# Gate weights loaded ahead of the second half of chunk 1's decay factors, and the steps of the first third in a new order

## The chip, the core and the metric

The kernel runs on one NeuronCore of a Trainium2 chip. That core has five engines, each with its own in-order instruction queue: TensorE (PE, matrix products), VectorE (DVE), ScalarE (ACT), GpSimd (POOL) and SyncE (SP, which here only issues DMAs). POOL both computes and issues DMAs. The metric is the device time of one execution in microseconds; the number of a kernel is the median of its runs.

## The reference

Two stages follow each other. The first is a gated linear recurrence over 768 positions, for 4 sequences with 8 heads of width 48; the second is a bilinear feed-forward layer over the 3072 tokens that come out of it.

```python
for t in range(S):                                     # S = 768
    state = alpha[:, :, t, :, None] * state + einsum('bhd,bhe->bhde', k[:, :, t], v[:, :, t])
    y[:, :, t] = einsum('bhd,bhde->bhe', q[:, :, t], state)
x = y.transpose(0, 2, 1, 3).reshape(B * S, H * D)      # 3072 x 384
a = x @ w_a                                            # 384 x 1536
b = x @ w_b                                            # 384 x 1536
out = (a * b) @ w_out                                  # 1536 x 384
```

## The kernel before

**Tiling.** The work is cut into six chunks, 0 to 5. A chunk is two of the four sequences (called u = 0 and u = 1) times 256 positions, 128 rows with a pair of positions in each. Chunks 0 and 1 are the first 256 positions of all sequences, 2 and 3 the next, 4 and 5 the last. Within a chunk the recurrence is computed in two halves g = 0 and 1 of 64 rows: logarithms of alpha are summed by a triangular matrix product, exponentials of the sums scale q and k, scores are formed, masked and multiplied with v, and the state carried from before is added. After that the chunk's 512 tokens go through the feed-forward layer, in 12 slices f of 128 columns of each of w_a and w_b.

**What sets the order.** No scheduler does. One string, `PROGRAM` (line 17), lists every step by hand in the form `chunk: step; step; ...`, and each engine gets its own steps in that order. A step waits for the data that it reads, and for the buffers and PSUM banks that it writes to be free; whatever stands behind it on its engine waits too. The last letter of many steps names the engine (V DVE, S ACT, P POOL, Y SP). A number at the end of a PE step is its PSUM bank (0 to 7); some steps take that bank and the next one.

The steps that matter here:

- `ld x u E`: DMA of chunk's a (alpha), q, k or v for u (`*` both, 0a/0b half the heads) from engine E's queue. `W a lo hi`, `W b lo hi`, `Wo lo hi`: DMA of columns of w_a, w_b, slices of w_out, all on POOL's queue.
- `ln u` (ACT, L554): logarithm of alpha. `l2 u P` (L562): sum of the two logarithms of a pair. `H`, `L` (DVE, L599, L605) and `R` (L621): splits of it into parts for PE. `B u` (PE, L589 and L590, two banks), `A2` (L636), `AQ` (L631, two banks): the running sums. `E u i`, `E u b` (ACT, L665): exponentials. `ra` (ACT, L643), `lv` (L650): scalings with single decay factors.
- `mk`, `mq` (DVE, L676): scaled k and q. `C u h` (PE, L736): their transposes; `Ce` (L960 on DVE, L958 on ACT): out of PSUM. `D u h` (PE, L837, two banks): scores; `M` (DVE, L846), or `Mc` (ACT, L850) and `Mm` (DVE, L854): scores masked.
- `dk` (PE, L698) and `de` (ACT, L719): decay over half a chunk. `K u g`, `K2` (PE, L792, L805): contribution of k and v to the state. `k u g V` (DVE, L819; L822 and L823 for g = 1): the new state.
- `v`, `vs` (L769 or L771; L958 or L960): v cast and its rows swapped. `SB`, `Y`, `SA` (PE, L866): the chunk's output, in two banks; `X` (L902 on ACT, L904 on DVE) takes it out as the input of the feed-forward layer.
- `a f u`, `b f u` (PE, L921): a slice of x @ w_a or x @ w_b for the tokens of u, three products over 256 columns, or of both (`*`), three over 512. `as` (ACT, L927) copies the a slice out of PSUM, into one of three buffers; `pr` (DVE, L935) multiplies it with the b slice. `o m half` (PE, L943): half of the product with w_out for 128 tokens; `ot` (L958) and `st`: out.
- `cz`, `cs`, `c2`, `c3`, `cm`, `ci`, `cu`: constants and zeros, mostly on POOL.

Chunks overlap: while chunk 0 is in its feed-forward layer, chunk 1's alphas, keys and queries go through ACT, DVE and POOL, and chunk 2's inputs are loaded. Around the change the DMA order on POOL's queue was: chunk 0's v, a, k, q for u = 1, then `W b 0 256`, `ld v 1`, `W a 256 768`, `W a 0 256`, `W b 256 512`, `W b 512 768`, chunk 1's `ld a 0` and `ld a 1`, `W a 768 1536`, `W b 768 1536`, chunk 1's `ld q 0`, `ld k 0`, `ld v 0`, `l2 0 P` (a computation), `ld q 1`, `Wo 0 6`, `l2 1 P`, `lv 0 q P`, `ld k 1`, `Wo 6 12`, then chunk 2's `ld a *` and so on.

Of the kernel before, what the change touches and what calls it, by code (L numbers as in the profile page):

```python
# [55 lines left out]
0: a 8 * 6; pr 5 1; pr 10 *
1: E 0 b
0: a 7 * 0; b 7 * 2
1: mq 0 V
0: b 11 * 4  # L60
2: ld k * P
1: lv 0 k V; E 0 i; mk 0 V
0: as 11 *; pr 11 *; a 6 * 3; as 7 *
1: A2 1 0
3: ld v * P
1: E 1 b
0: cz 1 v P; c3 P; pr 7 *
1: E 1 i
0: as 6 *; pr 6 *
1: dk * 7; de *  # L70
0: a 9 * 5; as 9 *; b 8 * 0
1: C 0 1 7; mq 1 V; Ce 0 1 V; C 0 0 2
0: b 9 * 1; pr 9 *; o 2 0 3; as 8 *; pr 8 *
1: Ce 0 0 S; D 0 0 4; Mc 0 0; K2 0 0 2 6
0: o 0 0 7; o 3 0 0
1: k 0 0 V; k 0 1 V; SB 0 4
3: ld a * P
1: mk 1 V; D 0 1 1; M 0 1
0: o 3 1 -; ot 3 V; st 3 Y
1: v 0 S; vs 0 0 S; vs 0 1 S; Mm 0 0 V; C 1 1 6; Ce 1 1 V  # L80
2: ln *
0: o 0 1 -; ot 0 S
1: C 1 0 2; Ce 1 0 S; v 1 V; vs 1 0 S
0: o 1 0 0; o 1 1 -; ot 1 S
# [12 lines left out]
2: R 0
1: D 1 0 6; as 4 0; k 1 0 V
2: ra 0
1: SB 1 2  # L100
2: R 1
1: k 1 1 V
2: AQ 0; E 1 i; ld v * P; E 1 b
1: pr 2 0; a 10 0 4; as 10 0; a 7 0 5; M 1 0; a 1 0 6; Mm 1 1 V; b 4 0 7; pr 4 0; b 1 0 1; a 5 0 4; as 1 0
1: pr 1 0
2: lv 0 q P; E 0 b; dr
1: b 10 0 6; pr 10 0; a 6 0 7; as 7 0; b 7 0 1; pr 7 0; b 5 0 5; as 5 0
# [5 lines left out]
1: b 6 0 1
2: mk 1 V; E 0 i
1: as 6 0; a 0 0 0; b 0 0 7; pr 6 0; a 11 0 4; X 1 S; a 2 1 5; b 3 0 2; as 0 0; pr 0 0; as 11 0; a 3 0 3
1: as 3 0; a 8 0 4; b 9 0 0; b 2 1 1; a 6 1 3; pr 11 0; as 2 1; a 9 0 5; as 9 0; pr 3 0; o 2 0 2
3: ln *; l2s 0 P; l2 0 P
0: st 0 Y
1: a 5 1 5; pr 2 1
2: lv 0 k V  # L120
1: as 8 0; a 8 1 1; as 8 1; b 8 0 6; a 3 1 7; pr 9 0; a 10 1 0
2: mk 0 V
1: pr 8 0
2: T 1
1: b 8 1 4; pr 8 1; b 5 1 1
2: dl
1: as 5 1; pr 5 1
3: l2s 1 P
1: as 6 1; b 6 1 6; pr 6 1; as 3 1; b 3 1 3; pr 3 1
# [1048 lines left out]
```

## Time and profile before

| what | value |
|---|---|
| median of 3 runs | 188.94 us (188.89 to 191.47) |
| the profiled execution: its own time | 190.44 us |
| the profiled execution: span from first to last instruction | 188.7 us |
| mean granted clock of TensorE | 0.991 |
| DVE busy | 152.6 us (81% of the span) |
| ACT busy | 120.1 us (64%) |
| POOL busy | 53.6 us (28%) |
| DMA moved | 29.43 MB |

Times in the profile count from the first instruction of the execution. "Busy" of PE includes the time a product spends in the pipeline, so a busy PE need not be at its full rate; the distance between the starts of neighbouring products shows the rate. A line of the timeline gives the start, the duration, the engine, the code line and operation, the output and input tiles and the number of merged instructions; a bracket at its end gives the idle time of the engine before it and who ended that.

### The profile page before, as it was taken

What the parts mean: (1) busy time and instruction counts of PE and PEld (TensorE: products, weight loads), DVE (VectorE), ACT (ScalarE), POOL (GpSimd) and SP (SyncE); (2) the same over time, 40 slices, a digit from 0 to 9 for tenths busy, and PEclk for the clock granted to TensorE, in tenths of its full rate; (3) what the DMA queues carried; (4) which work ended last, traced back from release to release, by engine and by line L of the source; (5) the groups of instructions that cost most, each with busy time, mean ns of one, the idle gap of its engine ahead of it and who ended that gap; (6) DMA issues with size and microseconds to landing.
All of it is one profiled execution on the core that took longest, in us unless ns stands there. A gap on an engine that the chain in (4) does not pass through costs nothing.

```text
span 188.7 us, 6347 instructions
## 1 busy us (share of the span) xinstructions
PE 181.9 (96%) x2693; PEld 122.3 (65%) x2709; DVE 152.6 (81%) x271; ACT 120.1 (64%) x228; POOL 53.6 (28%) x74
## 2 busy tenths in 40 slices
PE   7979999999999999999999999999999999999993
PEld 3969886566778886754445644555457477565992
DVE  2484889788979799998889899999999945696862
ACT  4364865579995797797697949965980451526230
POOL 8999654998062240003500003300000000000000
PEclk9987999999999999999999999999999999999999
DMA  5999999999999899989999699939500102110053
GB/s 125 263 225 195 261 235 254 230 231 257 247 214 129 129 215 276 275 237 182 198 173 271 144 116 167 112 107 165 89 0 9 43 0 83 44 43 0 0 170 127
DMA packets 66285, 29.43 MB, mean 156 GB/s; under 512 B 55776, under 2 KB 64624, under 8 KB 66256
## 3 DMA queue, kind: packets, MB, share of 16 engines
q1 hardware_dynamic: 47488, 16.34, 41.2%
q0 software_dynamic: 18624, 12.58, 39.3%
q8 instruction: 21, 0.34, 0.7%
q10 hardware_dynamic: 144, 0.10, 0.2%
q14 instruction: 8, 0.07, 0.1%
HBM read 25.98 MB, written 4.74 MB: 163 GB/s over the span
## 4 chain that ended last, share of the span: by engine, by line
PE 90%; ACT 6%; issue 2%; DVE 1%
PE psum L921 47%; PE psum L943 12%; PE psum L1032 11%; PE psum L866 5%; PE psum L837 3%; PE psum L589 2%; PE psum L590 2%; PE psum L736 2%; PE psum L572 2%; ACT vx L958 2%; PE psum L631 1%; ACT la L554 1%; PE psum L792 1%; PE psum L805 1%; PE psum L698 1%
## 5 line engine op out<-in xcount | busy, mean ns | idle before, releaser
L921 PE MATMUL psum<-xT,wb_t 128*128 128x512 bf16 (+1 forms) x263 | 55.8, 336 | 0.5 <-issue 0.2
L921 PE MATMUL psum<-xT,wa_t 128*128 128x512 bf16 (+1 forms) x262 | 55.2, 335 | 0.5 <-issue 0.2
L921 PEld LDWEIGHTS <-wa_t 128*128 128x128 bf16 x270 | 25.7, 98 | 19.2 <-issue 0.5
L921 PEld LDWEIGHTS <-wb_t 128*128 128x128 bf16 x270 | 25.5, 98 | 18.4 <-issue 0.5
L943 PE MATMUL psum<-wo_t,prod 128*128 128x384 bf16 x144 | 26.1, 327 | 0.0
L958 ACT ACTIVATE ot<-psum 128x384 f32<-128x384 f32 (+1 forms) x23 | 11.2, 487 | 17.7 <-PE psum L1032 15.4
L650 POOL TENSOR_TENSOR q_t<-q_t,ra 128x384 f32<-128x384 f32 x6 | 6.4, 1072 | 53.6 <-ACT ra L643 31.1
L943 PEld LDWEIGHTS <-prod 128*128 128x128 bf16 x144 | 13.3, 98 | 8.3
L958 ACT ACTIVATE vx<-v_t 32x384 bf16<-32x384 bf16 x26 | 13.5, 521 | 1.5 <-DVE vx L771 1.1
L1032 PEld LDWEIGHTS <-prod 128*128 128x128 bf16 x144 | 12.0, 98 | 1.2
L850 ACT ACTIVATE m<-psum 128x768 bf16<-128x768 f32 x14 | 11.0, 810 | 2.3 <-PE psum L837 2.3
L676 DVE TENSOR_TENSOR QKp<-q_t,beta 128x768 bf16<-128x768 f32 x10 | 9.4, 952 | 1.9 <-ACT beta L665 1.6
L554 ACT ACTIVATE la<-a_t 128x1536 f32<-128x1536 f32 (+2 forms) x9 | 9.5, 1054 | 1.7 <-DMA a_t<-in_alpha_dram 1.5
L676 DVE TENSOR_TENSOR QKp<-k_t,invb 128x768 bf16<-128x768 f32 x10 | 10.1, 1013 | 0.3
L846 DVE TENSOR_TENSOR m<-psum,mask 128x768 bf16<-128x768 f32 x10 | 9.5, 949 | 0.6 <-PE psum L837 0.6
L1044 DVE TENSOR_TENSOR ot<-psum,ot 128x384 f32<-128x384 f32 x9 | 5.0, 555 | 5.9 <-issue 3.2
L866 PE MATMUL psum<-m,vx 64*64 64x128 bf16 (+1 forms) x576 | 8.7, 205 | 0.0
L547 POOL DMA_DIRECT2D v_t<-in_v_dram x8 | 8.5, 1064 | 0.0
L866 PE MATMUL psum<-kqT,Sm 64*64 64x128 bf16 x144 | 7.5, 220 | 0.4 <-DVE Sm L819 0.4
L866 PEld LDWEIGHTS <-vx 64*64 64x64 bf16 x576 | 7.6, 108 | 0.1
L854 DVE TENSOR_TENSOR m<-m,mask 128x768 bf16<-128x768 bf16 x14 | 7.4, 550 | 0.0
L665 ACT ACTIVATE prod<-psum 128x384 f32<-128x384 f32 x8 | 3.5, 488 | 6.0 <-PE psum L590 6.0
(292 smaller groups left out, 361.5 us busy)
## 6 DMA issues: line engine op xcount, KB each, us to landing
out_dram<-ot SPq DMA_DIRECT2D x23, 192.0 KB, 2.7
q_t<-in_q_dram SPq DMA_DIRECT2D x3, 768.0 KB
k_t<-in_k_dram SPq DMA_DIRECT2D x3, 768.0 KB
a_t<-in_alpha_dram POOLq DMA_DIRECT2D x2, 768.0 KB, 11.7
v_t<-in_v_dram POOLq DMA_DIRECT2D x4, 384.0 KB, 7.6
a_t<-in_alpha_dram SPq DMA_DIRECT2D x2, 768.0 KB
a_t<-in_alpha_dram POOLq DMA_DIRECT2D x3, 384.0 KB, 7.5
k_t<-in_k_dram POOLq DMA_DIRECT2D x3, 384.0 KB, 7.3
```

The lines of the kernel that those rows point to most:

```text
L547: eng.dma_start(out=t[:, us, hs].rearrange("p b h r d -> p (b h) (r d)"), in_=src[ch.b0 + us.start:ch.b0 + us.stop, hs, ch.s * 2 * C:(ch.s ...
L554: nc.scalar.activation(out=ch.la[:, us, hs].rearrange("p b h r d -> p (b h r d)"), in_=ch.a[:, us, hs].rearrange("p b h r d -> p (b h r d) ...
L650: eng.tensor_mul(x, x, by)
L676: eng.tensor_mul(QKp[ch.c % 2][:, u, j, :, hs, :D], src[:, u, hs].rearrange("p h r d -> p r h d"), f)
L846: nc.vector.tensor_mul(m, x, maskn())
L850: nc.scalar.activation(out=m, in_=x, func=AF.Copy)
L854: eng.tensor_mul(m, m, maskn())
L866: nc.tensor.matmul(o, lhsT=lhsT, rhs=rhs, start=(g, c) not in begun, stop=False, skip_group_check=True)
L921: nc.tensor.matmul(p, lhsT=(wa_t, wb_t)[w][:, kk, f * 128:(f + 1) * 128], rhs=ch.xT[:, kk, us, :], start=(kk == 0), stop=(kk == KT - 1))
L943: nc.tensor.matmul(op, lhsT=ch.prod[:, f, at:at + C], rhs=wo_t[:, f, :], start=(f == 0), stop=(f == NFF - 1))
L958: nc.scalar.activation(out=o_, in_=i_, func=AF.Copy)
L1032: nc.tensor.matmul(o[:, g], lhsT=A[:, f, g * C:(g + 1) * C], rhs=W[:, f], start=(not more and (apart or g == 0) and f == 0), stop=(f == LH ...
```

## The change

The set of 893 steps is the same in both programs. `PROGRAM` is new between its third line and the step `o 2 0 2` of chunk 1's feed-forward layer: order and PSUM banks of the steps, on PE, ACT and DVE. From there to the end the program is unchanged but for some banks. On POOL's queue two things move: `W a 0 256` goes ahead of `W a 256 768`, and chunk 1's `ld a 1` goes behind `W a 768 1536`, `c2 P` and `W b 768 1536`. SP's queue keeps its order. In chunk 0, `K 0 1` and `dk 1` go ahead of chunk 0's running sums for u = 1 (`B 1a`, `B 1b`), and `ln 1` goes ahead of `vs 0 0 S`; in chunk 1, u = 0 goes ahead of u = 1 in more steps than before.

```diff
-0: E 0b i; mk 0b V; ld k 1 P; ld q 1 P; cm 1; W b 0 256; cz 0 v P; E 0b b; mq 0b V; ld v 1 P; W a 256 768; dk 0 2
-0: C 0 1 3; E 0a i; mk 0a V; cz 1 q P; E 0a b; mq 0a V; v 0 S; Ce 0 1 V; fill 2 0; W a 0 256; de 0; W b 256 512
-0: C 0 0 1; Ce 0 0 V; D 0 1 2; K 0 0 0; vs 0 0 S; W b 512 768; cs 1 m P
+0: E 0b i; mk 0b V; ld k 1 P; ld q 1 P; cm 1; W b 0 256; cz 0 v P; E 0b b; mq 0b V; ld v 1 P; W a 0 256; dk 0 2
+0: C 0 1 3; E 0a i; mk 0a V; cz 1 q P; E 0a b; mq 0a V; v 0 S; Ce 0 1 V; fill 2 0; C 0 0 4; Ce 0 0 V; D 0 1 0
+0: M 0 1; de 0; W a 256 768; K 0 0 3; D 0 0 5; k 0 0 V; K 0 1 2; ln 1; dk 1 4; de 1; vs 0 0 S; SB 0 0
+0: B 1a 3; E 1a i; k 0 1 V; M 0 0; vs 0 1 V; E 1a b; B 1b 5; W b 256 512; E 1b i; mk 1a V; mq 1a V; C 1 0 7
+0: Y 0; SA 0; mk 1b V; E 1b b; K 1 0 2; W b 512 768; mq 1b V; cs 1 m P
 1: ld a 0 P
-0: D 0 0 4; k 0 0 V; SB 0 0; M 0 0; ln 1; B 1a 6
-1: ld a 1 P
-0: W a 768 1536; c2 P; W b 768 1536; E 1a i; E 1a b; B 1b 4
-1: ld q 0 P
-0: dk 1 6
-1: ld k 0 P
-0: vs 0 1 V; E 1b i; M 0 1; Y 0; mk 1a V; mq 1a V; mk 1b V; SA 0; E 1b b; mq 1b V; C 1 0 7; Ce 1 0 V
-0: K 1 0 2; C 1 1 3; de 1; k 1 0 V; Ce 1 1 V
...
+0: C 1 1 3; Ce 1 0 V; v 1 S; vs 1 1 V; vs 1 0 V; D 1 0 4; X 0 S; b 1 0 7; Mc 1 0; a 1 0 6; as 1 0; b 0 0 0
+0: a 3 0 1; a 2 0 4; Ce 1 1 V; D 1 1 5; as 3 0; k 1 0 V; SB 1 1; K 1 1 3; as 2 0; a 0 0 4; pr 1 0; a 5 0 7
+0: Mm 1 0 V; k 1 1 V; Mc 1 1; Mm 1 1 V; a 4 0 3; b 3 0 5; W a 768 1536; pr 3 0; SA 1; as 5 0; Y 1; b 5 0 5
+0: b 4 0 6; b 2 0 7; X 1 V; as 0 0; pr 5 0; a 2 1 4; pr 2 0; c2 P; a 3 1 1
+1: ln 0
+0: W b 768 1536; pr 0 0; as 2 1; a 4 1 2; as 4 1; b 4 1 7; b 2 1 0; pr 2 1; b 3 1 4; b 0 1 2; as 3 1; pr 3 1
+0: a 0 1 1; b 1 1 0; b 5 1 4; as 4 0; pr 4 0; a 1 1 3
+1: ra 0
+0: pr 4 1; as 0 1; pr 0 1; a 7 * 5; a 5 1 1; as 5 1; a 11 * 6; b 7 * 7; b 10 * 1
+1: ld a 1 P; ld q 0 P; ld k 0 P
+0: as 1 1; b 11 * 2; as 11 *
+1: ld v 0 P; l2 0 P
+0: a 10 * 3; pr 5 1; a 9 * 4; as 7 *
+1: H 0 V; L 0 V; ld q 1 P; A2 0 5
...
+1: ln 1
+0: as 10 *; pr 7 *; pr 10 *
+1: E 0 b
...
 2: ln *
...
+1: SA 0; Mm 0 0 V; Y 0
...
+1: X 0 S; a 4 0 3
+0: ot 0 S
...
```

The steps of chunk 1 and 2 on ACT now read: `Ce 1 0 S`, chunk 2's `ln *`, chunk 1's `X 0 S`, `ot 0 S`. Before, chunk 2's `ln *` stood ahead of `ot 0 S` and `Ce 1 0 S`.

More of the change, by code (lines that the diff above doesn't have):

```diff
@@ L61 @@
+1: L 1 V; mq 0 V; A2 1 2; mk 0 V; ld k 1 P
+0: Wo 6 12; as 9 *
+1: C 0 1 4
+0: as 6 *; pr 9 *
+2: ld a * P
+0: as 8 *
+1: ra 1; ld v 1 P
+0: pr 8 *
+1: Ce 0 1 V; de *
+0: o 2 0 0
+1: E 1 i
+0: pr 6 *
+2: ld q * P
+1: lv 1 q P; lv 1 k P
 2: ld k * P
-1: lv 0 k V; E 0 i; mk 0 V
-0: as 11 *; pr 11 *; a 6 * 3; as 7 *
-1: A2 1 0
+1: E 1 b; K2 0 0 1 2
 3: ld v * P
[L66 to L72, printed above, removed]
@@ L102 @@
[L102 to L107, printed above, removed]
+1: Mc 1 1; a 2 0 1
+0: o 1 0 4
+1: k 1 0 V
+2: R 0
+0: o 1 1 -; ot 2 S
+1: b 2 0 0; as 2 0; vs 1 0 S; k 1 1 V
+0: ot 1 S
+1: D 1 0 1
+2: R 1; ra 1; AQ 5
+1: pr 2 0; as 4 0
+2: E 1 b; E 0 b; lv 1 q P
+1: SB 1 3; a 10 0 0; as 10 0; a 1 0 7
@@ L113 @@
[L113 to L117, printed above, removed]
+1: as 2 1; a 9 0 1; as 9 0; o 2 0 2
+3: ln *
+1: pr 11 0
+2: dr
+3: l2s 0 P; l2 0 P
 0: st 0 Y
-1: a 5 1 5; pr 2 1
+1: a 5 1 3; pr 2 1
 2: lv 0 k V
-1: as 8 0; a 8 1 1; as 8 1; b 8 0 6; a 3 1 7; pr 9 0; a 10 1 0
+1: as 8 0; a 8 1 1; as 8 1; b 8 0 0; a 3 1 7; pr 9 0; a 10 1 6
```

92 lines of the change are left out of this document (36 added, 56 removed).

## The prediction

> **What bounds the kernel now.** I read the page first, then the waits of PE, then the windows and the timelines of the engines up to 60 us.
>
> ```profile
> span 188.7 us, 6347 instructions
> ...
> PE 181.9 (96%) x2693; PEld 122.3 (65%) x2709; DVE 152.6 (81%) x271; ACT 120.1 (64%) x228; POOL 53.6 (28%) x74
> ...
> PE 90%; ACT 6%; issue 2%; DVE 1%
> ```
>
> PE is busy for 96% of the span and carries 90% of the chain that ended last. Since a busy PE need not be at its full rate, the rate has to be read from starts in the timeline:
>
> ```profile
> 20.68 0.83 PE L921 MATMUL psum<-xT,wa_t 128*128 128x256 bf16 x6
> ...
> 27.42 0.49 PE L921 MATMUL psum<-xT,wb_t 128*128 128x256 bf16 x3
> ...
> 27.75 0.49 PE L921 MATMUL psum<-xT,wa_t 128*128 128x256 bf16 x3
> ...
> 34.62 1.46 PE L921 MATMUL psum<-xT,wb_t 128*128 128x512 bf16 x6
> ...
> 35.92 0.81 PE L921 MATMUL psum<-xT,wa_t 128*128 128x512 bf16 x3
> ...
> 42.30 2.12 PE L943 MATMUL psum<-wo_t,prod 128*128 128x384 bf16 x12
> ```
>
> From 20.68 us PE works for the feed-forward layer. Three products over 256 columns take 27.75 - 27.42 = 0.33 us, six over 512 take 35.92 - 34.62 = 1.30 us, that is 0.65 for a whole slice. These prices, 0.33 for half a slice and 0.65 for a whole one, hold wherever such groups follow each other, so PE runs at its rate and not in the shadow of something else. `o` costs (2.12 for twelve with the pipeline's tail) about 1.0 per half. What PE lacked is short:
>
> ```profile
> PE psum L572 <- DVE og L472: 1.2, 1, 1.2
> PE psum L837 <- ACT bl L719: 0.5, 1, 0.5
> PE psum L866 <- DVE Sm L819: 0.4, 1, 0.4
> PE psum L589 <- ACT la L554: 0.4, 1, 0.4
> ```
>
> The first lies at the start, the other three between 9.5 and 12.6 us, 1.3 us together. After that PE practically never waits. So the change cannot win behind 20.68 us: with the same 893 steps PE can only start the feed-forward work earlier, and can lose wherever its new order waits. The first stretch has one more loss, the clock:
>
> ```profile
> 12.50:13.00 0.50, 0.47 (x2) 0.47 (x3) 0.46 (x3) 0.00 (x0) 0.50 (x2) 0.73 1.16 179
> ...
> 15.50:16.00 0.50, 0.50 (x3) 0.50 (x2) 0.13 (x1) 0.50 (x2) 0.50 (x1) 0.50 1.27 206
> ...
> 16.00:16.50 0.50, 0.50 (x4) 0.50 (x4) 0.50 (x2) 0.21 (x1) 0.50 (x2) 0.86 1.28 197
> ```
>
> The granted clock (the number after POOL's) is 0.73 on the mean in 12.5 to 13, where it falls to one half, still 0.50 in 15.5 to 16, and 0.86 in 16 to 16.5, where it comes back.
>
> **The change, part by part.** The sum is made on the profiled execution, 188.7 us of span within 190.44 us. The median of the runs is 188.94; I add the sum to the median, since a delay of PE passes from the one to the other unchanged.
>
> *The loads of weights.* `W a 0 256` goes out one issue earlier, `W a 256 768` one later. No row shows PE waiting for weights at 20.68, and the first reader of the moved columns (`a 3 0`) is the fourth slice. Nothing either way; the cover is what chunk 0 does before 20.68, and it would be gone if that stretch became over a microsecond shorter.
>
> *Before the feed-forward layer.*
>
> ```profile
> 14.46 0.84 PE L590 MATMUL psum<-la,ut 128*128 128x192 f32 x2
> ...
> 16.27 0.49 PE L589 MATMUL psum<-la,ut 128*128 128x192 f32 x2
> ...
> 16.59 0.49 PE L590 MATMUL psum<-la,ut 128*128 128x192 f32 x2
> ...
> 17.01 0.91 PE L698 MATMUL psum<-og,la 128*48 128x2 f32 x32
> ...
> 25.09 0.42 PE L792 MATMUL psum<-v_t,QKp 64*64 64x48 bf16 x15
> ```
>
> ```profile
> 10.19 0.34 ACT L719 ACTIVATE bl<-psum 48x8 f32<-48x8 f32 x2
> ...
> 10.55 1.06 ACT L958 ACTIVATE vx<-v_t 32x384 bf16<-32x384 bf16 x2
> ...
> 11.63 0.84 ACT L554 ACTIVATE la<-a_t 128x768 f32<-128x768 f32 x1
> ```
>
> `dk 1` (17.01, 0.84 until the next step at 17.85) and `K 0 1` (0.36 from 25.09 to 25.45) move into the 1.3 us of waits. `D 0 1` gets banks that no longer wait for `de 0`, the 0.5 us in the waits. In exchange `dk 1` waits for `ln 1`, which now follows `de 0` at 10.53 instead of two swaps (1.06). Its data were there at the latest at 11.63, where it started without a wait for them; between 10.53 and 11.63 I take 10.9, so `ln 1` ends at 11.75 and `dk 1` at 12.6. Behind it `de 1` (0.35) must empty bank 4 before `B 1a` may write it: 12.95 instead of 12.53, 0.4 later. Sixteen sums follow at 0.32 each under the half clock, 0.163 after it (the starts 16.27 to 16.59 are two). If the clock returns at the same time, they end about 0.2 later than before, at 17.1 instead of 16.9. Then `dk 1` is no longer in the way.
>
> ```profile
> 18.11 0.64 DVE L676 TENSOR_TENSOR QKp<-q_t,prod 128x384 bf16<-128x384 f32 x1
> ...
> 19.32 0.69 DVE L960 COPY kqT<-psum 128x1024 bf16<-128x1024 bf16 x1 [0.56 <-PE psum L736]
> ...
> 20.24 0.69 DVE L960 COPY kqT<-psum 128x1024 bf16<-128x1024 bf16 x1
> ...
> 20.96 1.41 DVE L960 COPY vx<-v_t 32x384 bf16<-32x384 bf16 x4
> ...
> 24.34 0.35 DVE L822 TENSOR_TENSOR tmp<-psum,Sm 128x192 f32<-128x192 f32 x1
> ...
> 24.72 0.36 DVE L823 TENSOR_TENSOR S<-tmp,bl 128x192 bf16<-128x192 f32 x1
> ...
> 25.31 0.96 DVE L904 CAST xT<-psum 128x768 bf16<-128x768 f32 x1 [0.23 <-PE psum L866]
> ```
>
> `mq 1b` ended at 18.75, now 18.95; `Ce 1 0` idled for PE's transpose before, and can now follow at once, to 19.65; `D 1 0` 0.3, and PE begins its first slice at 19.95 instead of 20.68. `X 0`, which the slice needs,
>
> ```profile
> 18.77 0.81 ACT L902 ACTIVATE xT<-psum 128x768 bf16<-128x768 f32 x1 [0.46 <-PE psum L866]
> ```
>
> ended at 19.58 and now stands behind `v 1 S` instead of ahead of it; with the output steps earlier by `dk 1`'s 0.84 and 0.8 of `v 1 S` in front, it ends at about 19.8, just in time. At 19.95 `K 1 1` is not done and `K 0 1` is, 0.36 each, so the work is equal: **-0.75**. Bounds: nothing, if `X 0` comes late; -1.2, if all of the old waits are filled.
>
> *DVE's order in chunk 0, 20 to 26 us.* The four swaps (1.41) now stand ahead of `Ce 1 1` (0.69): 19.65 + 1.41 + 0.69 = 21.75. PE reaches `D 1 1` after five half slices, at 21.6: 0.15. `k 1 0` (0.36 like its neighbours) at 22.1 lets `SB 1` go 0.05 late. `a 4 0` takes the bank of `K 1 1`, so it waits for `k 1 1`: after `pr 1 0` and `Mm 1 0`, some 0.85 together, the two steps of it (0.72) end at 23.65, PE is there at 23.3: 0.35. `X 1` (0.96) holds `a 2 1` by 0.1. Together **+0.65**, which gives back nearly all; bounds 0 (before, none of these waits exists) and 0.9.
>
> *The long way of chunk 1's second alphas.* `ld a 1` leaves POOL about 2 us later, behind both large weight loads. The nearest row for its landing is `q 0`, issued at 19.08 behind the same five transfers:
>
> ```profile
> q_t<-in_q_dram POOLq DMA_DIRECT2D x1, 384.0 KB, 12.5
> ```
>
> It landed at 31.6; `a 1` goes out ahead of it and has one transfer fewer in front, so 31.6 is its upper bound. That is not what decides: `ln 1` of chunk 1 now stands on ACT behind `as 7 *`. PE reaches the end of `a 11 *` at 19.95 + 0.65 + 24 half slices (7.9) + 2 whole (1.3) + 1.55 for `D 1 1`, `SB`, `SA`, `K 1 1`, `Y 1` = 31.35; two copies of 0.6 and `ln 1` (0.84) end at 33.4. Behind `ln 1` waits `l2 1` on POOL, and behind that, in POOL's queue:
>
> ```profile
> 28.17 1.00 POOL L562 TENSOR_TENSOR l<-la 128x384 f32<-128x384 f32 x1 [0.19 <-ACT la L554]
> ...
> 31.75 1.36 POOL L650 TENSOR_TENSOR q_t<-q_t,ra 128x384 f32<-128x384 f32 x1 [2.59 <-ACT as__707 L927]
> ...
> 33.06 0.95 POOL L547 DMA_DIRECT2D k_t<-in_k_dram  x1
> ...
> 34.82 1.18 POOL L547 DMA_DIRECT2D a_t<-in_alpha_dram  x1
> ```
>
> `l2 1` runs from 33.4 to 34.4 instead of 28.17 to 29.17, `lv 0 q` (1.36) to 35.75, then `ld k 1` at 35.75 instead of 33.06: **2.7 us later, and so all behind it**: `Wo 6 12`, chunk 2's alphas, `ld v 1`, chunk 2's q and k. Before, POOL waited 2.6 us ahead of `lv 0 q` (the row at 31.75); that wait is the cover, and it swallows 2.6 of the 5.2 us by which `l2 1` is later.
>
> Who feels it? On ACT, `as 10` stands behind `ln 1` (0.84), `pr 10` on DVE behind `as 10`, and DVE has no slack there:
>
> ```profile
> 36.00:40.00 4.00, 3.84 (x59) 2.76 (x59) 3.94 (x5) 2.67 (x7) 3.88 (x4) 1.00 1.15 206
> ```
>
> DVE is busy for 3.94 of 4 us, so up to 0.84 goes on to chunk 1's transposes and state steps, for which PE waits; I take **+0.6** (bounds 0, since PE has gate slices left, and 0.84). Next chunk 2's alphas:
>
> ```profile
> a_t<-in_alpha_dram POOLq DMA_DIRECT2D x1, 768.0 KB, 10.8
> ```
>
> ```profile
> 45.90 1.49 ACT L554 ACTIVATE la<-a_t 128x1536 f32<-128x1536 f32 x1
> ```
>
> They landed at 34.82 + 10.8 = 45.6, and `ln *` followed at 45.90. Now they land at 48.3 if the time to landing stays, and sooner if the transfers find an emptier queue. `ln *` (1.49) now stands ahead of `X 0` (0.81) on ACT: 48.3 + 1.49 + 0.81 = 50.6. PE gets to `a 4 0`, which needs `X 0`, after 18.3 us of work behind 31.35, with the 0.6 at 50.2: **+0.4** (bounds 0 and 1.0). Behind the same `ln *` DVE adds chunk 2's logarithms (three times 0.55), `k 1 0`, `k 1 1` and the two splits (0.95 each) before the sums `AQ`: 4.6 us after 49.8 is 54.4, PE is there at 54.1: **+0.3** (0 to 0.9).
>
> Sum: -0.75 + 0.65 + 0.6 + 0.4 + 0.3 = **+1.2**. Behind `o 2 0 2` of chunk 1 PE has the old order and no wait to win it back in, so all of it stays: 188.94 + 1.2 = 190.1.
>
> [...] The half clock lasted from about 12.7 to 16.1 us, after a stretch with 1.3 us of waits. [...]
>
> **The rivals.**
>
> *The clock stays up (0.2), not slower.* Its place is 12.5 to 17 us. For it: PE's waits in the three microseconds before are filled with 1.2 us of work. Against it: that work is products over 2 and 48 columns, which the half-empty stretch of before also had. Eleven sums would save 0.16 each, -1.75; the later terms stay, and some of the lead is lost again on loads that come at their own time: +1.2 - 1.75 is -0.55, about 188.4. It decides whenever less than 1.2 of lead is lost again. If no wait came either, -2.5.
>
> *The new waits don't come (0.17), not slower.* DMAs land sooner since less is in flight, and DVE and ACT make up their time in gaps: only -0.75 is left, 188.2. For it: the same stage before has no wait on PE at all. That the load order has no effect on landings, since all transfers share the DMA engines, comes out here too.
>
> *POOL's queue decides (0.13), slower.* The 2.7 us pass on whole, because `ld v 1` and `Wo 6 12` stand behind `ld k 1` and PE runs out of chunk 0's slices at about 45 us: +1.2 + 2.7 = 3.9, 192.8. It decides from the point where these transfers take as long to land as before although fewer are in flight; that they should is what speaks against it.
>
> **How the numbers follow.** My forecast, a small net loss, has 0.5; all low bounds together would give 187.7 and all high ones 192.6, which is unlikely for independent terms, so its own range goes about half the way down and two thirds up: 189.0 to 191.8. With the rivals, 8 in 10 lie from 187.9 to 192.2: below are the rare -2.5 and part of the kept clock, above most of the POOL rival. Two per cent (185.2 and 192.7) is about what a measurement of this kernel can tell from no change, the three runs lying 1.4% apart. Faster by more has 0.02, only with kept clock and no waits and still more; slower by more 0.11, nearly all of it POOL's rival; the rest, 0.87, lies within.
>
> **What would show it.** In the changed profile: the first `L921` product at about 20.0; the clock's 0.50 in 13 to 16 (if it is gone, the first rival); PE idle, or groups at more than 0.33 per half slice, near `D 1 1` and `a 4 0` at 21 to 24; `ld k 1` on POOL at about 35.8; `ln` of block 2's alphas (128x1536) at about 48, with PE waiting for `xT` behind it. If PE has no wait between 20 and 60, I am wrong about the order; if PE waits longer than 2 us at one place there, about POOL.

## The result and the profile after

| | before | after |
|---|---|---|
| median of 22 executions each, taken in turns | 189.55 us (188.44 to 195.11) | 191.45 us (190.43 to 194.02) |
| ratio, with its 95% interval | | 1.0107 [1.0079, 1.0135] |
| the profiled execution: its own time | 190.44 us | 191.41 us |
| the profiled execution: span | 188.7 us | 189.6 us |

The change costs 1.1%, some 2.0 us. The forecast was 1.2 us, so the sign held and the size was short. How the loss comes about is partly another story than the prediction's. The page of the changed kernel first:

```profile
span 189.6 us, 6358 instructions
...
PE 183.3 (97%) x2709; PEld 122.1 (64%) x2709; DVE 151.7 (80%) x271; ACT 120.2 (63%) x228; POOL 51.2 (27%) x74
...
PE 84%; ACT 5%; DMA 4%; DVE 2%; POOL 1%; issue 1%; POOLq 0%
```

PE is still what bounds the kernel. Its waits (engine, tile and line that waited, who ended the wait; us in total, times, longest) between 0 and 70 us:

```profile
PE psum L574 <- DVE og L474: 1.2, 1, 1.2
PE psum L839 <- DVE kqT L962: 0.7, 3, 0.3
PE psum L923 <- issue: 0.3, 1, 0.3
PE psum L700 <- ACT la L556: 0.2, 1, 0.2
```

All lines of code stand two further down than before. Of the three old waits at 9.5 to 12.6 us (1.3 us) 0.4 is left: one of the three on `kqT` and the one on `la`. The other two on `kqT` are new, and so is a gap that the view puts down to "issue": nothing that the profile shows ended it. PE's timeline has both (start, duration, work, idle time before it):

```profile
20.07 0.50 PE L923 MATMUL psum<-xT,wb_t 128*128 128x256 bf16 x3
...
22.16 0.37 PE L839 MATMUL psum<-kqT 64*64 64x128 bf16 x16 [0.28 <-DVE kqT L962]
...
22.81 0.61 PE L923 MATMUL psum<-xT,wa_t 128*128 128x256 bf16 x4
23.77 0.72 PE L923 MATMUL psum<-xT,wa_t 128*128 128x256 bf16 x5 [0.35 <-issue]
...
25.55 1.16 PE L923 MATMUL psum<-xT,wb_t 128*128 128x256 bf16 x9
```

The first gate product starts at 20.07, 0.61 earlier than before. The gap at 23.77 falls after one of the three products of a slice, and a slice needs nothing new between its products. The last row shown begins with the 28th gate product, which is product 412 of PE's stream (counted from 0; some records are missing from a trace, so numbers of products here hold to within three) in both kernels, with the same work behind it. Before, that product started at 25.45. So PE was 0.6 us early at the start of the slices and 0.1 late nine half slices on. The clock was as forecast (columns: window, length, five engines, then the granted clock):

```profile
13.00:13.50 0.50, 0.50 (x4) 0.50 (x3) 0.50 (x1) 0.48 (x2) 0.50 (x1) 0.52 1.56 182
...
15.50:16.00 0.50, 0.50 (x3) 0.50 (x2) 0.00 (x0) 0.06 (x1) 0.50 (x2) 0.50 1.37 203
16.00:16.50 0.50, 0.50 (x3) 0.50 (x3) 0.04 (x1) 0.50 (x2) 0.45 (x2) 0.57 1.29 207
```

POOL's queue slipped as forecast too (the key load at 35.95, 35.75 was the forecast):

```profile
34.03 0.99 POOL L564 TENSOR_TENSOR l<-la 128x384 f32<-128x384 f32 x1 [4.73 <-ACT la L556]
...
35.95 0.94 POOL L549 DMA_DIRECT2D k_t<-in_k_dram  x1
36.88 0.94 POOL L532 DMA_DIRECT2D wo_t<-in_moe_w_out_dram  x1
```

And `ln *` of chunk 2 started at 47.77 on ACT (48.3), with `X 0` behind it:

```profile
47.77 1.49 ACT L556 ACTIVATE la<-a_t 128x1536 f32<-128x1536 f32 x1
49.16 0.79 ACT L904 ACTIVATE xT<-psum 128x768 bf16<-128x768 f32 x1
```

But the slice that needs `X 0` started with no wait at all, at 50.36 on PE, and so did the sums `AQ` at 53.58:

```profile
50.36 0.82 PE L923 MATMUL psum<-xT,wa_t 128*128 128x256 bf16 x6
...
53.58 0.34 PE L633 MATMUL psum<-l,utb 64*64 64x384 bf16 x4
```

So the chain of late loads is there and does not reach PE in this execution. From the 28th gate product to the last product, PE's lag on before grows from 0.1 to 0.3 us; 0.6 of the 0.9 us between the two spans lies behind the last product. There the last store is left, which is issued from ACT's queue; the first line is before, the second after:

```profile
185.85 0.37 ACTq L1050 DMA_DIRECT2D out_dram<-ot  x1
...
186.15 1.19 ACTq L1052 DMA_DIRECT2D out_dram<-ot  x1
```

The issue takes 0.82 us longer. It took 0.37 us in all five profiles of programs with the old start, and 0.63 to 1.32 in the seven with the new start that were not padded. The prediction has no term for that stretch, and nothing was run on it.

### The profile page after: what moved, and what is told of

It reads as the page before. It is cut to its first block, busy times and chain, and to the rows that moved or that the text cites. A ratio compares the mean times of both kernels' runs of the same rounds, so it can differ in the third digit from the quotient of the medians.

```text
span 189.6 us, 6358 instructions
## 1 busy us (share of the span) xinstructions
PE 183.3 (97%) x2709; PEld 122.1 (64%) x2709; DVE 151.7 (80%) x271; ACT 120.2 (63%) x228; POOL 51.2 (27%) x74
## 4 chain that ended last, share of the span: by engine, by line
PE 84%; ACT 5%; DMA 4%; DVE 2%; POOL 1%; issue 1%; POOLq 0%
PE psum L923 46%; PE psum L945 12%; PE psum L1034 11%; PE psum L868 5%; DMA a_t<-in_alpha_dram 4%; PE psum L839 3%; PE psum L591 1%; PE psum L633 1%; ACT la L556 1%; ACT vx L960 1%; PE psum L807 1%; PE psum L592 1%; PE psum L738 1%; PE psum L700 1%; DVE vx L962 1%
## 5 line engine op out<-in xcount | busy, mean ns | idle before, releaser
L678 DVE TENSOR_TENSOR QKp<-k_t,invb 128x768 bf16<-128x768 f32 x10 | 9.5, 952 | 0.5 <-ACT as__1864 L929 0.5
L868 PE MATMUL psum<-m,vx 64*64 64x64 bf16 (+1 forms) x576 | 8.6, 205 | 0.0
L678 DVE TENSOR_TENSOR QKp<-k_t,prod 128x384 bf16<-128x384 f32 x4 | 2.4, 591 | 5.9 <-ACT prod L667 5.8
```

The lines of the kernel that those rows point to most:

```text
L678: eng.tensor_mul(QKp[ch.c % 2][:, u, j, :, hs, :D], src[:, u, hs].rearrange("p h r d -> p r h d"), f)
L868: nc.tensor.matmul(o, lhsT=lhsT, rhs=rhs, start=(g, c) not in begun, stop=False, skip_group_check=True)
```

## The experiments

**First four: which part of the new order.** Two theories stood against each other: the prediction's (losses on DVE at 21 to 24 us, and behind the late loads at 35 to 54 us) and that the gap without a releaser carries the loss. Both kernels were run again, and two mixtures.

*Before, again.*

> The kernel before, once more with a profile. If the difference of the two kernels is one of order, its PE reaches chunk 1's running sums AQ, chunk 2's K2 and the last product at the times of the first profile, within 0.3 us. If it is the state of the clock that counts, a profile without the 0.50 stretch between 12.5 and 16.5 us is possible, and then everything behind 17 us comes about 1.7 us earlier.

Measured: 189.08 us, span 187.3. In this execution the half clock did not come at all (windows):

```profile
13.00:13.50 0.50, 0.50 (x5) 0.50 (x5) 0.47 (x3) 0.00 (x0) 0.50 (x2) 1.00 1.91 212
...
15.50:16.00 0.50, 0.50 (x26) 0.50 (x23) 0.23 (x2) 0.50 (x2) 0.50 (x2) 1.00 1.24 202
```

That goes with 188.7 - 187.3 = 1.4 us, so traces have to be compared at like clock. PE's timeline, with the start of the slices, a short gap without a releaser, and the 28th gate product:

```profile
18.91 0.83 PE L921 MATMUL psum<-xT,wa_t 128*128 128x256 bf16 x6
...
23.14 0.68 PE L866 MATMUL psum<-m,vx 64*64 64x128 bf16 x45 [0.19 <-issue]
...
24.03 0.50 PE L921 MATMUL psum<-xT,wa_t 128*128 128x256 bf16 x3
```

*After, again.*

> The changed kernel, once more. Theory 1 (the new order loses by waits of PE behind 20 us): 1.0 to 2.5 us over the kernel before, and the waits near 22 and 23.5 us are there again. Theory 2 (the clock's stretch is only caught more often by the changed kernel): executions of the two kernels with the same clock differ by less than 0.5 us.

Measured: 190.82 us, ratio 1.0084 [1.0057, 1.0111]. The profile is of the longest of the six executions (193.32 us, with the half clock). The gap stands at the same product and is longer, and PE now waits once for output weights:

```profile
24.66 0.72 PE L923 MATMUL psum<-xT,wa_t 128*128 128x256 bf16 x5 [1.17 <-issue]
...
46.84 1.14 PE L945 MATMUL psum<-wo_t,prod 128*128 128x384 bf16 x6 [0.80 <-DMA wo_t<-in_moe_w_out_dram]
```

The second theory fails: the five executions without the half clock have a median of 190.74 us, 1.8 over the 188.93 of the kernel before.

*The changed start with the old order behind it.* Up to the transposes of u = 1 the steps stand as in the changed kernel, behind them and in the queue of loads as before:

```diff
-0: C 0 1 3; E 0a i; mk 0a V; cz 1 q P; E 0a b; mq 0a V; v 0 S; Ce 0 1 V; fill 2 0; W a 0 256; de 0; W b 256 512
...
+0: C 0 1 3; E 0a i; mk 0a V; cz 1 q P; E 0a b; mq 0a V; v 0 S; Ce 0 1 V; fill 2 0; C 0 0 4; Ce 0 0 V; D 0 1 0
+0: M 0 1; de 0; W a 0 256; K 0 0 3; D 0 0 5; k 0 0 V; K 0 1 2; ln 1; dk 1 4; de 1; vs 0 0 S; SB 0 0
+0: B 1a 3; E 1a i; k 0 1 V; M 0 0; vs 0 1 V; E 1a b; B 1b 5; W b 256 512; E 1b i; mk 1a V; mq 1a V; C 1 0 7
+0: Y 0; SA 0; mk 1b V; E 1b b; K 1 0 2; W b 512 768; mq 1b V; cs 1 m P
...
-0: Mm 1 1 V; SA 1; Y 1; K 0 1 6; pr 2 0; a 4 0 0; as 4 0; b 5 0 7; k 1 1 V; a 5 0 4; X 1 V; a 1 1 2
+0: Mm 1 1 V; SA 1; Y 1; pr 2 0; a 4 0 0; as 4 0; b 5 0 7; k 1 1 V; a 5 0 4; X 1 V; a 1 1 2
```

> The new order up to the transposes of chunk 0's u = 1 (dk 1, K 0 1 and ln 1 early), the old order and the old loads behind. Theory 1: as fast as before or up to 0.8 us faster, since the first gate product starts at about 20.0 and the waits behind are the old ones. Rival (the early part itself loses, by B 1a behind ln 1, dk 1 and de 1): 0.3 to 1 us slower.

Measured: 190.52 us, ratio 1.0104 [1.0069, 1.0140]. The start alone is as slow as the whole change. PE starts the slices at 20.01, 0.67 early as the expectation has it, and loses all of it and more in one gap, again within a slice:

```profile
20.01 0.83 PE L918 MATMUL psum<-xT,wa_t 128*128 128x256 bf16 x6
...
24.96 0.39 PE L918 MATMUL psum<-xT,wb_t 128*128 128x256 bf16 x2 [2.01 <-issue]
```

*The old start with the new order behind it.* `K 0 1` stays early, in a bank that the running sums overwrite before its result is read, so the state behind chunk 0 is partly another one; only its time is read. The loads are those of before, and behind `C 1 1` comes the order of the changed kernel.

```diff
-0: C 0 0 1; Ce 0 0 V; D 0 1 2; K 0 0 0; vs 0 0 S; W b 512 768; cs 1 m P
+0: C 0 0 1; Ce 0 0 V; D 0 1 2; K 0 0 0; K 0 1 7; vs 0 0 S; W b 512 768; cs 1 m P
...
-0: vs 0 1 V; E 1b i; M 0 1; Y 0; mk 1a V; mq 1a V; mk 1b V; SA 0; E 1b b; mq 1b V; C 1 0 7; Ce 1 0 V
+0: vs 0 1 V; E 1b i; M 0 1; k 0 1 V; Y 0; mk 1a V; mq 1a V; mk 1b V; SA 0; E 1b b; mq 1b V; C 1 0 7; Ce 1 0 V
...
```

> The old order up to the transposes of chunk 0's u = 1 with the old loads (only K 0 1 early), the new order of steps behind. Theory 1: the whole loss and the early gain's absence, 1.5 to 2.8 us slower than before. Rival (the loss comes from the order of the loads): within 0.5 us of the kernel before.

Measured: 190.60 us, ratio 1.0076 [1.0048, 1.0103]. It too has the gap, and a wait for output weights:

```profile
22.62 0.71 PE L929 MATMUL psum<-xT,wa_t 128*128 128x256 bf16 x5 [0.73 <-issue]
...
44.89 1.14 PE L951 MATMUL psum<-wo_t,prod 128*128 128x384 bf16 x6 [0.90 <-DMA wo_t<-in_moe_w_out_dram]
```

The two halves of the change do not add up (each alone costs 0.8 to 1.0%, both 0.8 to 1.1%), as if both paid for one and the same thing, though in the profile of the second half the output weights (0.90) cost more than the gap (0.73). Counting PE's records in the traces shows the common part: **in each of the five traces that have the gap it stands at product 350 or 351 of PE's stream, and at the 356th weight load, whatever work that product belongs to**: in `Y 1` before, in a gate slice after. And the list of DMA queues has one that carries instructions (packets, MB, share of the engines; here from 21 to 24 us of the changed start with the old order):

```profile
q8 instruction: 1, 0.02, 2.6%
```

Over the whole execution it has 21 packets and 0.34 MB, 16 KB each. The page of the changed kernel counts 2709 products and as many weight loads. If the packets carry these, each has 2709 / 21 = 129 products with their weight loads on the mean; taken as 128, that is the estimate of a block from here on. The new theory: PE runs out of instructions at a block's border, because the next block comes too late.

The packets' own times in the traces fit it. Columns: when PE started product 242, some 20 into the block that begins at 222 (to within 0.1 us); when the packet behind it started, and how long it took; when PE resumed at 350 or 351.

| kernel | product 242 | packet | resumed | from 242 to that |
|---|---|---|---|---|
| before (no gap of its own: 350 at 24.44) | 19.27 | 22.04 + 1.25 | | |
| before, again | 17.45 | 20.51 + 1.21 | 23.14 | 5.7 |
| after | 18.34 | 21.53 + 0.94 | 23.77 | 5.4 |
| after, again | 18.65 | 22.32 + 0.95 | 24.66 | 6.0 |
| new start, old order | 18.30 | 22.21 + 1.24 | 24.96 | 6.7 |

From product 242 on PE has 108 products in hand and gets the next block 5.4 to 6.7 us later. In the first profile of before the work up to the border took 5.2 us (19.27 to 24.44) and just covered that. In the three profiles of changed kernels it took 4.7 to 5.1 us, since small products (`K 0 1`, 16 of them within 0.3 us) stand ahead of the border and gate products (0.11 us each) behind it; and the packet started 3.2 to 3.9 us behind product 242 instead of 2.8. So the gap has two parts, less work up to the border and a later packet. The order accounts for the first; why the packet came later is not shown.

**Second four: move the border, not the work.** 46 more products at the start, in time in which PE waits for the first alphas, shift every border by 46 products against the work.

*Before, with 46 products more.*

```diff
-0: cm 0; c1; cz 0 b P; ci; ld a 0b Y; c1a; ld a 0a Y; ln 0b; cu; cz 1 b P; fill 7 0; cu2 V
+0: cm 0; c1; cz 0 b P; ci; ld a 0b Y; c1a; ld a 0a Y; ln 0b; cu; cz 1 b P; fill 2 0; pad 51 0; cu2 V
...
+    def pad(n, i):
+        for _ in range(n):
+            nc.tensor.matmul(bank(i)[:32, :40], lhsT=wz[:, :32], rhs=wz[:, :40], start=True, stop=True)
```

> The kernel before, in which 5 of the 7 warming products at the start (128x512) give way to 51 products of 32x40: 46 more products in TensorE's stream, in time in which TensorE waits for the first alphas; no other step is touched. Theory of the instruction blocks (a block holds 128 products with their weight loads, its refill is to hand some 6.3 us after TensorE has crossed the block before): the boundary that lies at product 350 comes to the 304th product of the old count, which TensorE reaches about 3.4 us after the one before (176); so a gap of 2 to 2.7 us that nothing releases, some 20 products into the new stage at 21 to 24 us, and the time is 1.2 us to 2.5 us longer, ratio 1.006 to 1.013. Rival (the blocks do not matter, the change costs through DVE, ACT and the queues): ratio 1.000 within 0.002, gaps as before.

Measured: 194.93 us, ratio 1.0256 [1.0209, 1.0303]. The gap has moved to other work, the third product of a gate slice, and stands again at product 350 of the stream, old number 304:

```profile
20.62 0.38 PE L925 MATMUL psum<-xT,wa_t 128*128 128x256 bf16 x2
22.19 0.27 PE L925 MATMUL psum<-xT,wa_t 128*128 128x256 bf16 x1 [1.19 <-issue]
```

It is half as long as expected. The loss is twice what was expected, because there are more of them; PE's waits over the whole span have 4.2 us on "issue", where before had 0.3 (0.16 at 38.06 and at 129.24 us, and these are no waits: a weight load stands there whose product is missing from the records):

```profile
PE psum L870 <- issue: 2.3, 2, 1.7
PE psum L925 <- issue: 1.5, 3, 1.2
...
PE psum L635 <- issue: 0.4, 1, 0.4
```

Laid beside the profile of before with full clock, PE's lag is nearly constant but for steps at products 350, 862, 1373, 1756 and 2139: 1.4, 0.7, 0.3, 2.0 and 0.8 us. The distances are 512, 511, 383 and 383 products, four and three times 128 but for one. At the end the lag is 6.0 us (spans 193.3 and 187.3); 0.7 of it was there ahead of the first step, 0.44 of that a wait for gate weights.

*After, with 46 products more* (the same edit).

> The changed kernel with the same 46 products more at the start, and nothing else. Theory of the blocks: the boundary at product 350 (gap 0.35 us in one profile, 1.17 us in another) comes to 304, in front of which TensorE has taken 6 us and more for its block, and the next one to 432, about 6.6 us on: no gap of over 0.3 us is left before 30 us, and the time falls by 0.4 to 1.3 us, ratio to the kernel before 1.001 to 1.006 instead of 1.008 to 1.011. Rival (blocks do not matter): 1.008 to 1.011 as it is.

Measured: six executions from 192.79 to 198.56 us, with a median of 197.06; the ratio, 1.0268 [1.0202, 1.0333], rests on the two shortest. Neither theory holds. New gaps, at products 223 and 350 of the stream:

```profile
14.38 0.48 PE L595 MATMUL psum<-la,ut 128*128 128x192 f32 x1 [0.71 <-issue]
...
24.34 1.03 PE L927 MATMUL psum<-xT,wa_t 128*128 128x256 bf16 x4 [1.94 <-issue]
```

The expectation let the refill begin when PE crosses a border. The trace says that it begins later: PE crossed 222 at 13.3, then did slow sums, reached product 242 at 18.55, and the packet started at 22.09. So the 6 us count from some 20 products into the block rather than from its first; from which one exactly these traces do not fix.

*The changed start with the old order, with 46 products more.*

> The kernel with the changed start and the order and loads of before behind it (ratio 1.0104, a gap of 2.01 us at product 350), with the same 46 products more. Theory of the blocks: the gap of 2.0 us goes, what stays is the early start of the gate products (0.6 us), so 188.1 to 189.0 us, ratio 0.996 to 1.001. Rival (the gap is another wait, which the order brings): it stays, at the same product b 0 0, ratio 1.009 to 1.012.

Measured: a median of 199.5 us (195.7 to 201.5), too scattered for a ratio. Gaps at 223 and 350 again, 1.81 and 2.57 us. The expectation failed for the same reason, and padding is no remedy: it moves all later borders as well.

*After, with the load order of before.*

```diff
-0: E 0b i; mk 0b V; ld k 1 P; ld q 1 P; cm 1; W b 0 256; cz 0 v P; E 0b b; mq 0b V; ld v 1 P; W a 0 256; dk 0 2
+0: E 0b i; mk 0b V; ld k 1 P; ld q 1 P; cm 1; W b 0 256; cz 0 v P; E 0b b; mq 0b V; ld v 1 P; W a 256 768; dk 0 2
...
-0: M 0 1; de 0; W a 256 768; K 0 0 3; D 0 0 5; k 0 0 V; K 0 1 2; ln 1; dk 1 4; de 1; vs 0 0 S; SB 0 0
+0: M 0 1; de 0; W a 0 256; K 0 0 3; D 0 0 5; k 0 0 V; K 0 1 2; ln 1; dk 1 4; de 1; vs 0 0 S; SB 0 0
...
-1: ld a 0 P
+1: ld a 0 P; ld a 1 P
...
-1: ld a 1 P; ld q 0 P; ld k 0 P
+1: ld q 0 P; ld k 0 P
```

> The changed kernel with the load order of before (gate weights and block 1's alphas back in their places), the placing of the steps as changed. Prediction on record: the loads at the start cost nothing by themselves, so the ratio stays at 1.008 to 1.011. Theory of the blocks: the refill waits in the same DMA engines as the loads; an order with less queued at 18 to 22 us would bring it earlier, at most by the gap, 0.4 to 1.2 us: 1.003 to 1.009. A third reading, that the late loads of block 1 (third key load at 35.9 us instead of 33.1) carry the loss: ratio 1.000 to 1.005.

Measured: 190.79 us, ratio 1.0101 [1.0065, 1.0137], with the gap (1.25 us) at the same product. The load order by itself costs nothing that shows, as the prediction had it; the late loads of chunk 1 do not carry the loss, and the old order does not bring the refill sooner. At full clock it is 1.4 us over before (190.57, 4 executions, against 189.17) where the change has 1.8, so 0.4 may still lie there.

**Last four: a control, and two steps put back.**

*Before, with 128 products more*, one whole block, so that every border lies at its old work; the products have 24 columns instead of 40:

```diff
-0: cm 0; c1; cz 0 b P; ci; ld a 0b Y; c1a; ld a 0a Y; ln 0b; cu; cz 1 b P; fill 7 0; cu2 V
+0: cm 0; c1; cz 0 b P; ci; ld a 0b Y; c1a; ld a 0a Y; ln 0b; cu; cz 1 b P; pad 135 0; cu2 V
```

> Control for the padded kernels: the kernel before with all 7 warming products of the start (128x512) replaced by 135 products of 32x24, so 128 products more in TensorE's stream, one whole block. Theory of the blocks: every boundary lies at the same step as in the kernel before, so ratio 0.997 to 1.003, no gap of over 0.5 us at the old product 304, and the gaps at 0.1 to 0.5 us at the old product 350. Rival (more products at the start cost time in themselves, by the clock or by a late start): 128 cost at least what 46 did, ratio 1.025 or more.

Measured: 190.60 us, ratio 1.0070 [1.0045, 1.0096], outside of both expectations. The timeline tells why: the 135 products took until 4.89 us instead of 4.15, and the first sums ran at half their rate until 8.9 us instead of 6.1 (though the view of the clock reads 1.00 there in both), so that PE is 1.6 us late by the second sums.

```profile
1.19 3.77 PE L576 MATMUL psum<-wz 128*32 128x24 bf16 x135 [1.19 <-DVE og L472]
4.89 1.01 PE L593 MATMUL psum<-la,ut 128*128 128x192 f32 x2
...
20.62 0.83 PE L925 MATMUL psum<-xT,wa_t 128*128 128x256 bf16 x6
...
25.68 0.50 PE L925 MATMUL psum<-xT,wa_t 128*128 128x256 bf16 x3
```

The slices start 20.62 - 18.91 = 1.71 late, the 28th gate product is 25.68 - 24.03 = 1.65 late and the last product 1.7; there is no step in between, and PE's waits have nothing on "issue" over the whole span. So 128 more products make no gaps and 46 more make five: what counts is where the borders fall. The list of queues agrees with blocks of 128 products: one packet more than before (21, 0.34 MB), while 46 more products brought none.

```profile
q8 instruction: 22, 0.36, 0.8%
```

The late start is a fault of this control, and it is all of its loss.

*The changed start with the old order, `K 0 1` put back behind `Y 1`.* The step on DVE that reads it, `k 0 1`, goes back to its old place too.

```diff
-0: M 0 1; de 0; W a 0 256; K 0 0 3; D 0 0 5; k 0 0 V; K 0 1 2; ln 1; dk 1 4; de 1; vs 0 0 S; SB 0 0
+0: M 0 1; de 0; W a 0 256; K 0 0 3; D 0 0 5; k 0 0 V; ln 1; dk 1 4; de 1; vs 0 0 S; SB 0 0
...
-0: Mm 1 1 V; SA 1; Y 1; pr 2 0; a 4 0 0; as 4 0; b 5 0 7; k 1 1 V; a 5 0 4; X 1 V; a 1 1 2
+0: Mm 1 1 V; SA 1; Y 1; K 0 1 6; pr 2 0; a 4 0 0; as 4 0; b 5 0 7; k 1 1 V; a 5 0 4; X 1 V; a 1 1 2
...
```

> The kernel with the changed start and the order of before behind it (ratio 1.0104, gap 2.01 us at product 350), with one step put back: K 0 1, 16 products of 0.02 us, which fill an old wait there, goes back behind Y 1, where they cost 0.3 us of TensorE's time. Theory of the blocks: product 350 is now 16 products further on in the work, 1.06 us of gate products and unpacked sums by the trace, so the gap shrinks from 2.0 to about 1.0 us and the time by 0.5 to 0.8 us, ratio 1.005 to 1.008. Rival (the step's own place counts): the time grows by 0.3 us, ratio 1.010 to 1.013, and the gap stays at 2.0 us.

Measured: 190.48 us, ratio 1.0069 [1.0035, 1.0103], where it was 1.0104. Half of its 12 executions had the half clock and half had not. Among those with a mean clock of 0.995 or more the median went from 190.47 (4 executions, 190.43 to 190.56) to 189.77 (6, 189.10 to 190.31): 0.7 us faster, or 0.9 when each is taken against the kernel before in its own series (188.93 and 189.13), by a step that costs 0.3 us of work where it was put. The gap shrank from 2.01 to 0.47 and is back in `Y 1`:

```profile
19.06 0.83 PE L918 MATMUL psum<-xT,wa_t 128*128 128x256 bf16 x6 [0.44 <-DMA wa_t<-in_moe_w_a_dram]
...
23.56 0.68 PE L863 MATMUL psum<-m,vx 64*64 64x128 bf16 x44 [0.47 <-issue]
...
24.45 0.50 PE L918 MATMUL psum<-xT,wa_t 128*128 128x256 bf16 x3
```

The two gaps are not at like clock: the 2.01 is from an execution with the half clock, the 0.47 from one without, and the 0.44 us of waiting in the first row, ahead of the border, shortens it too. So it is the medians that carry the comparison. The moved DVE step does not explain it up to the slices: PE was ready for them at 19.06 - 0.44 = 18.62, and at 18.59 in the full-clock profile of the next kernel, which has `k 0 1` early.

The first row shows a second lid on the early start: without the half clock PE is there before the gate weights, and starts no earlier than before (18.91).

*After, with the second half of the output weights issued 3 us sooner.*

```diff
-0: b 9 * 0; Wo 0 6
+0: b 9 * 0; Wo 0 6; Wo 6 12
-0: Wo 6 12; as 9 *
+0: as 9 *
```

> The changed kernel with one DMA issue moved: the second half of the output weights is issued behind the first (some 33.9 us) instead of 3 us later (36.9 us). In one of two profiles of the changed kernel TensorE waited 0.8 us for these weights at 46.8 us, in the other not at all. Theory: that wait is gone in every execution, so 0.2 to 0.8 us less than the changed kernel, ratio 1.005 to 1.009; other waits as before. Rival (the weights are late only where the whole execution is late): 1.008 to 1.011 as it is.

Measured: 191.31 us, ratio 1.0103 [1.0069, 1.0136], not told apart from the change itself. At full clock the median is 190.39 (7 executions), against 190.74 and 190.91 for the change in two other series, so 0.3 to 0.5 us may lie there; the profile has no wait for these weights, which one of two profiles of the change did not have either. The gap remains:

```profile
23.00 0.72 PE L923 MATMUL psum<-xT,wa_t 128*128 128x256 bf16 x5 [0.82 <-issue]
```

*The same, with `K 0 1` put back behind `Y 1`*, and `k 0 1` behind `X 1`. `K 0 1` takes a bank in which half of chunk 0's output tile for u = 1 still stands, so this tile and what follows from it are other values; only its time is read.

```diff
-0: M 0 1; de 0; W a 256 768; K 0 0 3; D 0 0 5; k 0 0 V; K 0 1 2; ln 1; dk 1 4; de 1; vs 0 0 S; SB 0 0
+0: M 0 1; de 0; W a 256 768; K 0 0 3; D 0 0 5; k 0 0 V; ln 1; dk 1 4; de 1; vs 0 0 S; SB 0 0
...
-0: Mm 1 0 V; k 1 1 V; Mc 1 1; Mm 1 1 V; a 4 0 3; b 3 0 5; W a 768 1536; pr 3 0; SA 1; as 5 0; Y 1; b 5 0 5
+0: Mm 1 0 V; k 1 1 V; Mc 1 1; Mm 1 1 V; a 4 0 3; b 3 0 5; W a 768 1536; pr 3 0; SA 1; as 5 0; Y 1; K 0 1 2; b 5 0 5
...
```

> The kernel just described, and K 0 1 (16 products) put back behind Y 1. Theory of the blocks: product 350 comes 16 products, 1.07 us, further on in the work, so its gap (0.35 and 1.17 us in two profiles) is under 0.4 us; against the kernel with only the weights moved 0.2 to 0.8 us less, ratio 1.002 to 1.006. Rival (the step's place itself): 0.3 us more than that kernel.

Measured: 191.01 us, ratio 1.0087 [1.0055, 1.0119]; at full clock 190.09 against 190.39 (6 and 7 executions), with the half clock 191.47 against 192.15. So 0.3 to 0.7 us faster, as expected, though the intervals of the two ratios overlap. PE's waits in 0 to 70 us have no "issue" left (this profile has the half clock, that of the kernel without the step put back has not):

```profile
PE psum L574 <- DVE og L474: 1.2, 1, 1.2
PE psum L700 <- ACT la L556: 1.1, 1, 1.1
PE psum L839 <- DVE kqT L962: 0.4, 2, 0.2
PE psum L923 <- DVE prod L937: 0.2, 1, 0.2
```

No version beat the kernel before.

## Why the prediction was right in sign and short in size

The forecast was 188.94 + 1.2 = 190.1; the change cost 2.0 us by the ratio, and the median, 191.45, lies inside the range on record. That the sum comes so near is in part luck: in the profile of after, 0.35 of the 0.72 us lost between the start of the slices and the 28th gate product (0.65 was forecast) are a gap that it did not foresee, the 1.3 of the later terms came as 0.2, and 0.65 behind the last product was in no term.

*The early start, -0.75.* Right: -0.61 in the profile of after and -0.67 with the new start alone, both with the half clock. At full clock it is smaller, 18.59 against 18.91 in the kernel with the output weights moved, and nothing in the kernel that met the weights (19.06). The loads of the gate weights, taken as no term, can cap it: PE waited 0.44 us for them there, to 19.06, and as long in the kernel before with 46 products more, to 19.63.

*DVE's order in chunk 0, +0.65.* Its part at `D 1 1` was right and small: PE waited 0.28 us there in one profile and 0.52 in another, where the prediction had 0.15. **Its largest part failed**: "`a 4 0` takes the bank of `K 1 1`, so it waits for `k 1 1`", 0.35. No profile shows that wait. What stands there, 0.35 us long by chance, is the gap at the count of 350, by the theory PE out of instructions, and it was 1.17 us in the next profile. The prediction read PE's rate and its waits for others and left out a third way to be idle. The profile of before hardly showed it: the list of queues has a line on instructions, but no gap stands at the border, and the 0.3 us on "issue" are missing records.

*`as 10` behind `ln 1`, +0.6; `X 0` behind `ln *`, +0.4; `AQ`, +0.3.* The slips were forecast to within 0.7 us (34.03 for 33.4, 35.95 for 35.75, 47.77 for 48.3), but in the profile of after PE did not wait for any of them: from the 28th gate product to the last its lag grows by 0.2 us. **The steps from a late buffer to a waiting PE failed** there, most of all "up to 0.84 goes on to chunk 1's transposes", taken from DVE's busy time without a row in which PE waits for it. What the late queue did cost is the fourth item in it, `Wo 6 12`: 0.80 us in one of two profiles of the change, none in the other, and 0.90 with the old start. The prediction named `Wo 6 12` only under POOL's rival, with the whole 2.7. In some other profiles with the new order more of these terms comes true: against before at full clock the lag grows by 0.7 us over the same stretch in the kernel with the output weights moved (one wait of 0.16 for a state step on DVE is in it), and by 1.4 in the two profiles with a wait for output weights. So the later terms were not nothing in every execution; where the rest of the 0.7 goes was not followed.

*The clock.* The forecast took the half clock as given on both sides. It is not: of the executions whose clock the experiments list, 1 of 57 of the kernel before had a mean clock under 0.995 (its profile of the prediction, which had one of 0.991, is not among them); of the kernels with the changed start that were not padded, 22 of 54, and 9 of 22 in the series of the result; with the old start and the new order, none of 6. Each such execution is 1.4 to 1.8 us longer, by the medians of the two kinds (190.91 and 192.29 for the change in that series); the single one of the change run again is 2.6 longer. For the kernel before in the series of the result no clocks are listed, but six of its 22 executions took 190.66 us or more, as its known ones with the half clock did (190.44 and 190.96). So how much more often the changed start meets it is not settled.

The first rival, that work in the old waits keeps the clock up, did not hold: the changed start meets the half clock no less often than before, and in the experiments more often. That the waits ahead of the half clock bring it about was an estimate from one stretch, and no run shows it. Both kinds occur in one kernel: in 15.5 to 16 us the granted clock is 0.50 in the first profile of before and 1.00 in the next. What brings it about was not tried; the wait for `la` just ahead of the sums does not tell the two kinds apart (0.2 to 1.1 us in profiles with the half clock, 0.6 and 0.8 in two without).

*The sum as it was.* At full clock on both sides the change costs 190.74 - 188.93 = 1.8 us. By the medians, 0.7 to 0.9 of that hangs on `K 0 1` standing ahead of the border (new start, old order) and about 0.3 on the order behind the start (190.74 against 190.47), from 4 to 6 executions each; the rest, 0.6 to 0.8, is the new start without `K 0 1`. The full-clock profiles say where it is lost. In that of the new start without `K 0 1` (span 188.0, before 187.3) 0.1 is lost at the first slice, which waits for weights, 0.3 at the border and 0.3 behind the last product; its wait of 0.80 for `la` does not reach the slices. In that of the whole change with the output weights moved (188.9) PE is 0.3 early at the first slice and loses 1.1 by the 28th gate product (the gap of 0.82 and the wait of 0.52 at `D 1 1`), 0.7 from there to the last product and 0.2 behind it. So missing instructions are the largest single item, and not all of the loss. The half clock comes on top. Of the other rivals, "the new waits don't come" holds for 35 to 54 us in the profile of after alone and fails for 20 to 24, and of POOL's rival 0.8 to 0.9 us came, in two profiles, where it had 2.7.

What stays open: why a refill takes 5.4 to 6.7 us at 18 to 25 us. At a later border of the padded kernel it took less (product 1648 to the resumption at 1756: 3.5 us, with a DMA share of 0.70 at 104 to 109 us where 18 to 22 us have 1.21), so it took longer where more was loaded; that the loads are the cause is not shown, and a kernel with the loads taken out of that stage was not run. Open too is the long issue of the last store. A second instruction queue (q14) gives a hint: its last packet comes 1.3 to 1.6 us after that issue has begun in the five profiles of the old start, and 0.2 to 1.0 us before it in the seven of the new start that were not padded, so ACT may be short of instructions there as PE is at its borders.

## What to carry to other kernels

An idle time of PE within a group of products, which no semaphore ends, can be a sign of missing instructions: here such gaps of 0.19 to 2.57 us stood at product 350 or 351, whatever the work. See first that a weight load does not stand there, whose product is only missing from the records; then count the products to it, and see whether the count stays when the work moves. Where many small products follow each other, the order can have a price per product, beside the time that each takes: here blocks of 128 of them within 4.9 to 6.5 us left PE waiting 0.2 to 2.0 us, and filling an old wait with small products brought the border nearer. So try large products ahead of a border and small ones behind it (here 16 put back won 0.3 to 0.9 us, and no version beat the kernel before), and compare traces at like clock before looking for a step that is late.

## What the hardware showed beyond that

- Instructions came in packets of 16 KB on q8, 21 in an execution and 22 with 128 products more; gaps of PE stood at products 222, 350, 862, 1374, 1758 and 2142 of the stream, to within three. The packet for a border started 2.8 to 3.9 us after PE was some 20 products into the block before it, took 0.9 to 1.3 us, and PE resumed 1.3 to 1.5 us after its end, all at 18 to 25 us. The last figure holds for the later gaps of the padded kernel before too: packets that ended at 53.2, 107.9 and 131.7 us, PE back at 54.6, 109.2 and 133.1.
- 46 products of 0.034 us at a place where PE had nothing to do cost 6.0 us of span, 5.2 of it at five places up to 130 us later.
- A stretch at half clock at 12.5 to 16.5 us came in some executions of a kernel and not in others; where a gap of instructions of 1.81 us lay just ahead of it (the padded kernel with the changed start and the old order), the clock was still at 0.50 at 19 to 20 us.
- The issue of the last store on ACT's queue took 0.37 us in the five profiles with the old start and 0.63 to 1.32 us in the seven with the new one that were not padded; from the start of the last product to the end it was 3.5 us in the former and 3.6 to 4.2 in the latter.
